# Inverse row norm computed on 96 by 3 values, and attention priorities of batches 1 to 3 spread by VectorE and GpSimd work

## The chip, the core and the metric

The kernel runs on one core of one Trainium2 chip. The metric is the device time of one execution in microseconds (us); the time before is the median of three runs. Beside it stands one profiled execution, from which all rows below come. TensorE (PE) does matrix products, VectorE (DVE), ScalarE (ACT) and GpSimd (POOL) work on elements, SyncE (SP) issues nearly all DMAs.

## The reference

Nystrom attention on q, k, v of shape 4 x 8 x 576 x 64 (batch, head, token, dimension), then a gated MLP behind an RMS norm, then a second MLP, all in fp32, 2304 tokens of width 512:

```python
def _moe_ref(x, w_gate, w_val, w_out, rms_g):
    rms = np.sqrt(np.mean(x * x, axis=-1, keepdims=True) + 1e-06)
    xn = x / rms * rms_g
    g = xn @ w_gate
    silu = g * (1.0 / (1.0 + np.exp(-g)))
    val = xn @ w_val
    return (silu * val @ w_out)

def _moe2_ref(x, w_in, w_out, s, b):
    r = np.maximum(x @ w_in, 0.0)
    return ((s * (r * r) + b) @ w_out)

attn = A @ Z @ C @ v      # A, C softmaxes against 32 landmarks, Z from 6 steps Z = 2 Z - Z Bm Z
x = attn.transpose(0, 2, 1, 3).reshape(2304, 512)
out = _moe2_ref(_moe_ref(x))
```

The weights come as 64-bit floats and are narrowed on the chip.

## The kernel before

Four batches of 576 tokens. Batch 0's attention comes first (to about 41.7 us of the span). Then the first MLP runs in 48 units, counted from 0: each is one of 12 slices of 128 hidden columns for one batch, 12 units to a batch. While the units of batch b run, the attention of batch b + 1 is worked in between, so attention 1 lies in units 0 to 11, attention 2 in 12 to 23, attention 3 in 24 to 35. Units 36 to 47 have no attention; in them the second MLP's weights are narrowed. From 529 us on the second MLP runs alone.

A unit is, on PE: eight products of `fused` (L972, weights r times the folded attention matrix gw, into a PSUM bank), 24 products of `first_mm` (L991) and, six units later for the same slice, 24 products of `out_mm` (L1039; in the first 12 units plain fp32 products, L1035). Between them ACT copies the bank of L972 to `uh` (L978), DVE subtracts to get `ul` (L980); ACT takes the tanh (L1006), DVE multiplies (L1008, L1012). In units 0 to 11 the first MLP's weights are also loaded and narrowed: a DMA into one of three `stage` buffers (L884, L886), two ACT passes (L897, L899), two DVE passes (L901, L904), and a store for later batches.

At the end of each attention stands the row norm, once for each half of the batch (288 columns; 8 times in all). x is never written out there: `x_mm` (L821) makes each quarter of x transposed in a bank, ACT squares it (L827), in batches 1 to 3 two additions (L833, DVE or POOL) sum the quarters, and a product with a 128 x 128 matrix of ones (L839) puts the sum of squares into all 128 rows of a bank. Then DVE adds 1e-6 (L843) and takes the reciprocal (L844) of 128 x 288 values in place, ACT takes the root (L847), DVE scales the two halves of the attention probabilities by it (L852), ACT and POOL split these into `xh` and `xl` (L856, L858), which the first MLP's products of the next batch read. In batch 0 the four quarters are summed by four products in place of the additions.

The order of the work is made when the program is built. Each operation has a key (its priority) and a planned duration on each engine that may do it; `Scheduler.run` walks through planned time and gives an engine that is free the ready operation of lowest key. On the chip each engine then does its instructions in that fixed order and waits by semaphores. Keys of the units are their planned times `T[n]`. The keys of one batch's attention are set by `by_path` (L120 to L132): between `t0` and `t1`, the planned times of the units beside it, each operation stands by the length of the longest path behind it. Planned costs of POOL and DVE operations hold each other off where both use the memory port that the two share (`pair`). Until planned time 60, `warm` (L1228) puts small products with ones into gaps of PE, into bank 7.

The attention of batches 1 to 3 has two PSUM banks, 6 and 7 (`at_r`); a bank is taken at the first operation that uses it and given back after the last.

Of the kernel before, what the change touches and what calls it, by code (L numbers as in the profile page):

```python
# [14 lines left out]
ALU = mybir.AluOpType  # L15
# [69 lines left out]
class Scheduler:  # L85
# [38 lines left out]
    def by_path(self, ops, t0, t1):  # L124

        way, inside = {}, {id(o) for o in ops}
        for o in reversed(ops):
            way[id(o)] = min(o.alts.values()) + max(
                (self.CROSS + way[id(u)] for u in o.users if id(u) in inside), default=0.0)
        most = max(way.values())  # L130
        for o in ops:
            o.key = t1 - (t1 - t0) * way[id(o)] / most  # L132

# [109 lines left out]
def t_mm4(n):  # L243
    return 0.00167 * max(n, 120)
# [3 lines left out]
def tile_nystrom_attention_two_mlps(  # L248
# [152 lines left out]
    def attention(b, t0, t1):  # L401
# [406 lines left out]
        for hf in range(2):  # L808
# [3 lines left out]
            for c in range(KD):  # L812
# [12 lines left out]
                if pr == 0:  # L825
                    at(("pe", 0.6), p0, x_mm, r=[WBD, AT[hf, g]], w=[*pX2, (xq, "taken")])
                at(("act", t_act(HC)), p0 + 0.01, lambda e, c=c, pX=pX, xq=xq: e.activation(  # L827
                    out=xq.t[:, HC * c:HC * c + HC], in_=pX.t[:, 0:HC], func=ACTF.Square, scale=float(DM) ** -0.5),
                    r=[pX], w=[(xq, c)])
            pS = Buf(ps_r)  # L830
# [7 lines left out]
            for c in range(n_sum):  # L838
                at(("pe", t_mm4(HC)), p0 + 0.05, lambda e, c=c, pS=pS, xq=xq: nc.tensor.matmul(  # L839
                    out=pS.t[:, 0:HC], lhsT=ones, rhs=xq.t[:, HC * c:HC * c + HC],  # L840
                    start=(c == 0), stop=(c == n_sum - 1)), r=[(xq, c), "const"] + ([pS] if c else []), w=[pS])
            def s_rec(e, pS=pS):
                e.tensor_scalar(out=pS.t[:, 0:HC], in0=pS.t[:, 0:HC], scalar1=1e-6, scalar2=None, op0=ALU.add)  # L843
                e.reciprocal(out=pS.t[:, 0:HC], in_=pS.t[:, 0:HC])  # L844

            at(("dve", 2 * t_dve(HC)), p0 + 0.06, s_rec, r=[pS], w=[pS])
            at(("act", t_act(HC) if first else 1.3 + t_act(HC)), p0 + 0.07, lambda e, pS=pS: e.activation(  # L847
                out=pS.t[:, 0:HC], in_=pS.t[:, 0:HC], func=ACTF.Sqrt), r=[pS, "table"], w=[pS])
            for g in range(2):
                a = AT[hf, g]  # L850
                cols = slice(2 * HC * g + HC * hf, 2 * HC * g + HC * hf + HC)
                at(("dve", t_dve(HC)), p0 + 0.08, lambda e, a=a, pS=pS: e.tensor_tensor(  # L852
                    out=a.t[:, 0:HC], in0=a.t[:, 0:HC], in1=pS.t[:, 0:HC], op=ALU.mult), r=[a, pS], w=[a])
# [239 lines left out]
    EARLY = 15  # L1093
    units = [(b, f) for b in range(B) for f in range(F1)]
# [64 lines left out]
    for n in range(len(units) + HALF + 1):  # L1159
        t = T[n]  # L1160
        if n < len(units):
            b, f = units[n]
            if f == 0:
                if b + 1 < B:
                    attention(b + 1, *at_time(b + 1))
                    S_.by_path(batch_ops[b + 1], *at_time(b + 1))
                else:
# [97 lines left out]
```

## Time and profile before

| | |
|---|---|
| time, median of 3 runs | 922.77 us (922.74 to 926.39) |
| the profiled execution's own time | 924.32 us |
| its span, first to last instruction | 922.3 us |
| PE, DVE, ACT, POOL busy | 881.8, 722.4, 444.9, 124.1 us |
| mean granted clock of TensorE | 0.990 of full |

Busy shares are means over stages with different limits. PE's instructions overlap, so a busy PE says that it had work, and an idle stretch of PE is work time lost. The granted clock of a stretch is a mean of two levels, 1.0 (2.4 GHz) and 0.5 (1.2 GHz).

### The profile page before, as it was taken

The numbers are of one execution on the slowest core, as the hardware profiler recorded it, in microseconds if no ns is written. First come the engines' busy times: TensorE is split into PE (matmuls) and PEld (weight loads), VectorE is DVE, ScalarE is ACT, GpSimd is POOL, SyncE is SP. The second block draws the span as 40 slices with busy tenths as digits, with TensorE's granted clock in tenths as the row PEclk, the third lists the DMA queues.
The fourth block names the chain that finished last, engine by engine and source line by source line (L and its number), as shares of the span: only waits on it lengthen the run. The fifth ranks groups of instructions, "written<-read, shape, count | busy, mean of one in ns | idle before, by whom it ended". The sixth has DMA issues, their size and how long they took to land.

```text
span 922.3 us, 16186 instructions
## 1 busy us (share of the span) xinstructions
PE 881.8 (96%) x6077; PEld 734.5 (80%) x6077; DVE 722.4 (78%) x1454; ACT 444.9 (48%) x885; POOL 124.1 (13%) x154
## 2 busy tenths in 40 slices
PE   8778998999989999999899999999999999999998
PEld 5565766898868988798788888888888888888896
DVE  7878888887898878888989966676667666666686
ACT  5466657434553345556767333343334334333454
POOL 1550053500850004200000000000000000000000
PEclk9989998999999999999999999999999999999999
DMA  7778878873524433348876200010001000100010
GB/s 222 197 231 282 279 223 271 289 255 92 144 85 143 131 101 91 94 145 268 288 253 220 74 0 1 1 46 1 0 1 46 1 1 0 47 1 1 18 30 23
DMA packets 72126, 105.92 MB, mean 115 GB/s; under 512 B 25200, under 2 KB 45680, under 8 KB 72048
## 3 DMA queue, kind: packets, MB, share of 16 engines
q1 hardware_dynamic: 71856, 104.62, 36.2%
q8 instruction: 48, 0.79, 0.3%
q14 instruction: 30, 0.25, 0.1%
q10 hardware_dynamic: 192, 0.26, 0.1%
HBM read 90.70 MB, written 14.16 MB: 114 GB/s over the span
## 4 chain that ended last, share of the span: by engine, by line
PE 76%; DVE 11%; DMA 5%; issue 3%; ACT 3%; SPq 0%; DVEq 0%; ACTq 0%
PE bank L1065 21%; PE bank L955 21%; PE bank L991 13%; PE bank L1039 10%; PE bank L972 3%; DVE cmag L901 2%; DMA stage<-in_moe_w_val_dram 2%; PE bank L1035 2%; DMA stage<-in_moe_w_out_dram 1%; PE bank L642 1%; PE bank L1228 1%; PE bank L580 1%; DVE wl L873 1%; DMA region<-in_q_dram 1%; DVE rawg L904 1%
## 5 line engine op out<-in xcount | busy, mean ns | idle before, releaser
L991 PE MATMUL bank<-xh,uh 128*128 128x288 f32 x384 | 127.1, 331 | 14.6 <-DVE ul L980 12.9
L955 PE MATMUL bank<-xh,uh 128*128 128x512 f32 (+1 forms) x320 | 117.7, 368 | 1.0 <-ACT hbuf L1206 1.0
L955 PE MATMUL bank<-xl,uh 128*128 128x512 f32 (+1 forms) x320 | 117.6, 368 | 0.0
L955 PE MATMUL bank<-xh,ul 128*128 128x512 f32 (+1 forms) x320 | 117.6, 368 | 0.0
L1206 ACT ACTIVATE hbuf<-bank 128x512 f32<-128x512 f32 (+1 forms) x79 | 44.0, 556 | 149.5 <-PE bank L955 147.5
L991 PE MATMUL bank<-xl,uh 128*128 128x288 f32 x384 | 114.5, 298 | 0.0
L991 PE MATMUL bank<-xh,ul 128*128 128x288 f32 x384 | 114.4, 298 | 0.0
L1065 PE MATMUL bank<-wh,hh 128*128 128x512 f32 x288 | 112.4, 390 | 0.3 <-DVE hh L872 0.3
L1065 PE MATMUL bank<-wl,hh 128*128 128x512 f32 x288 | 112.3, 390 | 0.0
L1065 PE MATMUL bank<-wh,hl 128*128 128x512 f32 x288 | 112.0, 389 | 0.0
L991 PEld LDWEIGHTS bank<-xh,uh 128*128 128x128 f32 x384 | 73.3, 191 | 40.1 <-DVE ul L980 16.8
L1039 PE MATMUL bank<-hh,wh 128*128 128x288 f32 x336 | 101.1, 301 | 0.0
L1039 PE MATMUL bank<-hl,wh 128*128 128x288 f32 x336 | 99.6, 296 | 1.0 <-DVE hl L873 1.0
L1039 PE MATMUL bank<-hh,wl 128*128 128x288 f32 x336 | 99.0, 295 | 0.0
L873 DVE TENSOR_TENSOR hl<-hbuf,hh 128x512 fp32r<-128x512 f32 (+2 forms) x126 | 73.6, 585 | 2.4
L991 PEld LDWEIGHTS bank<-xl,uh 128*128 128x128 f32 x384 | 73.7, 192 | 0.7
L991 PEld LDWEIGHTS bank<-xh,ul 128*128 128x128 f32 x384 | 73.5, 191 | 0.0
L955 PEld LDWEIGHTS bank<-xh,uh 128*128 128x128 f32 x320 | 60.2, 188 | 12.6 <-ACT hbuf L1206 1.2
L955 PEld LDWEIGHTS bank<-xl,uh 128*128 128x128 f32 x320 | 60.0, 188 | 11.0
L872 DVE CAST uh<-region 128x512 fp32r<-128x512 f32 x57 | 24.3, 426 | 56.7 <-PE bank L955 56.7
L955 PEld LDWEIGHTS bank<-xh,ul 128*128 128x128 f32 x320 | 60.1, 188 | 10.0
L1039 PEld LDWEIGHTS bank<-hh,wh 128*128 128x128 f32 x336 | 63.2, 188 | 3.6 <-issue 2.1
(188 smaller groups left out, 1849.0 us busy)
## 6 DMA issues: line engine op xcount, KB each, us to landing
rawo<-kepto SPq DMA_DIRECT2D x84, 256.0 KB, 3.3
rawg<-keptg SPq DMA_DIRECT2D x36, 512.0 KB, 3.7
stage<-in_moe_w_out_dram SPq DMA_DIRECT2D x28, 512.0 KB, 4.9
stage<-in_moe_w_in_dram SPq DMA_DIRECT2D x16, 512.0 KB, 5.4
stage<-in_moe_w_gate_dram SPq DMA_DIRECT2D x12, 512.0 KB, 4.9
stage<-in_moe_w_val_dram SPq DMA_DIRECT2D x12, 512.0 KB, 5.4
keptg<-rawg SPq DMA_DIRECT2D x12, 512.0 KB, 6.2
region<-in_k_dram SPq DMA_DIRECT2D x8, 576.0 KB, 5.8
```

The lines of the kernel that those rows point to most:

```text
L580: nc.tensor.matmul(out=ps.t[p, pn * g:pn * g + n], lhsT=lhsT(p, g), rhs=rhs(p, g), start=True, stop=True)
L642: nc.tensor.matmul(out=ps.t[:, 0:HC], lhsT=part(u, "bd")[:, 128 * e:128 * e + 128], rhs=part(y, "t").rearrange("p (t e i) -> p t e i", e=2 ...
L872: else e.tensor_copy(out=hi(), in_=src())), r=r, w=[wh], pair=True)
L873: b = op({"dve": t_dve(n), "pool": t_pool(n)}, key, lambda e: e.tensor_tensor(out=lo(), in0=src(), in1=hi().bitcast(F32), op=ALU.subtract) ...
L901: op(("dve", t_dve(512)), key, lambda e: e.scalar_tensor_tensor(out=m.t, in0=word(1), scalar=-2 ** 31, in1=m.t, op0=ALU.bitwise_and, op1=A ...
L955: nc.tensor.matmul(out=ps.t[:, 0:n], lhsT=w[a].t[:, ks], rhs=x[y].t[:, kd, 0:n], start=(kd == 0 and i == 0), stop=(kd == KD - 1 and i == 2))
L972: nc.tensor.matmul(out=pU.t[64 * i:64 * i + 64, 256 * g:256 * g + 256], lhsT=gw[b].t[:, 64 * k:64 * k + 64], rhs=r.t[:, :, 128 * k:128 * k ...
L991: nc.tensor.matmul(out=ps.t[:, 0:HC], lhsT=u[a].t[:, 256 * g + 128 * part:256 * g + 128 * part + 128], rhs=x[y].t.rearrange("p k n -> p (k ...
L1035: nc.tensor.matmul(out=A[c].t[:, 0:HC], lhsT=r.t[:, 128 * c:128 * c + 128], rhs=h.t, start=(f == 0), stop=(f == F1 - 1))
L1039: nc.tensor.matmul(out=A[c].t[:, 0:HC], lhsT=w[a].t[:, 128 * c:128 * c + 128], rhs=hs[y].t[:, 0:HC], start=(f == 0 and i == 0), stop=(f == ...
L1065: nc.tensor.matmul(out=A[c].t, lhsT=hs[a].t[:, s], rhs=w[y].t, start=(f == 0 and i == 0), stop=(f == F2 - 1 and i == 2))
L1206: e.activation(out=r.t[:, 0:n], in_=ps.t[:, 0:n], func=ACTF.Relu) if e is nc.scalar
```

## The change

Two edits.

The norm: the sums of squares are now wanted once for each token, as 96 rows by 3 columns, in place of 128 equal rows by 288 columns. For each of three groups of 96 tokens a product takes the squares as the stationary matrix (128 x 96) and one column of ones as the moving one, so the sum of squares of a token falls into one of 96 partitions (`s_mm`; 3 products, in batch 0 four times as many). Scaling by 1/512 moves from the square's scale to the DVE instruction that adds 1e-6. That instruction, the reciprocal and the root work on 96 x 3 values, now in SBUF. To get the result back into 128 rows by 288 columns, DVE or POOL multiplies a 96 x 96 identity by the three columns (`dg`, 96 x 288), and one product of ones with it (contraction over 96) spreads each value over all 128 rows of a second bank, pR. The scaling reads pR.

The keys: after `by_path`, `by_work` moves the keys of the attention of batches 1 to 3 seven tenths of the way (`EVEN`) to a place that grows evenly with the DVE and POOL work done so far. The order within one attention by key stays; its place against the units' work changes. Nothing else is edited, but all orders are made anew.

```diff
@@ -130,6 +130,17 @@
         most = max(way.values())
         for o in ops:
             o.key = t1 - (t1 - t0) * way[id(o)] / most
+
+    def by_work(self, ops, t0, t1, part):
+
+
+        def work(o):
+            return 0.1 + (o.alts["dve"] if "dve" in o.alts else 0.6 * o.alts.get("pool", 0.0))
+
+        total, done = sum(work(o) for o in ops), 0.0
+        for o in sorted(ops, key=lambda o: o.key):
+            o.key += part * (t0 + (t1 - t0) * done / total - o.key)
+            done += work(o)
 
     def start_of(self, o, e):
         t = max((f + (self.SAME if d == e else PEC if e == 'pe' and o.key > 5 else self.CROSS) for d, f in o.ready.items()), default=0.0)
@@ -825,9 +836,8 @@
                 if pr == 0:
                     at(("pe", 0.6), p0, x_mm, r=[WBD, AT[hf, g]], w=[*pX2, (xq, "taken")])
                 at(("act", t_act(HC)), p0 + 0.01, lambda e, c=c, pX=pX, xq=xq: e.activation(
-                    out=xq.t[:, HC * c:HC * c + HC], in_=pX.t[:, 0:HC], func=ACTF.Square, scale=float(DM) ** -0.5),
-                    r=[pX], w=[(xq, c)])
-            pS = Buf(ps_r)
+                    out=xq.t[:, HC * c:HC * c + HC], in_=pX.t[:, 0:HC], func=ACTF.Square), r=[pX], w=[(xq, c)])
+            pS, pR, rs, dg = Buf(ps_r), Buf(ps_r), Buf(sm_r), Buf(a_ring)
             if not first:
                 for c, n in ((2, 2 * HC), (1, HC)):
                     at(dp(n), p0 + 0.03, lambda e, c=c, n=n, xq=xq: e.tensor_tensor(
@@ -835,22 +845,36 @@
                         r=[(xq, i) for i in range(KD)] if n > HC else [(xq, 0), (xq, c)],
                         w=[(xq, 0)] + ([(xq, 1)] if n > HC else []))
             n_sum = KD if first else 1
-            for c in range(n_sum):
-                at(("pe", t_mm4(HC)), p0 + 0.05, lambda e, c=c, pS=pS, xq=xq: nc.tensor.matmul(
-                    out=pS.t[:, 0:HC], lhsT=ones, rhs=xq.t[:, HC * c:HC * c + HC],
-                    start=(c == 0), stop=(c == n_sum - 1)), r=[(xq, c), "const"] + ([pS] if c else []), w=[pS])
-            def s_rec(e, pS=pS):
-                e.tensor_scalar(out=pS.t[:, 0:HC], in0=pS.t[:, 0:HC], scalar1=1e-6, scalar2=None, op0=ALU.add)
-                e.reciprocal(out=pS.t[:, 0:HC], in_=pS.t[:, 0:HC])
-
-            at(("dve", 2 * t_dve(HC)), p0 + 0.06, s_rec, r=[pS], w=[pS])
-            at(("act", t_act(HC) if first else 1.3 + t_act(HC)), p0 + 0.07, lambda e, pS=pS: e.activation(
-                out=pS.t[:, 0:HC], in_=pS.t[:, 0:HC], func=ACTF.Sqrt), r=[pS, "table"], w=[pS])
+
+            def s_mm(_, pS=pS, xq=xq):
+                for j in range(3):
+                    for c in range(n_sum):
+                        nc.tensor.matmul(
+                            out=pS.t[0:NP, j:j + 1], lhsT=xq.t[:, HC * c + NP * j:HC * c + NP * j + NP],
+                            rhs=ones[:, 0:1], start=(c == 0), stop=(c == n_sum - 1))
+
+            at(("pe", 0.26 * n_sum), p0 + 0.05, s_mm, r=[*[(xq, c) for c in range(n_sum)], "const"], w=[pS])
+
+            def s_rec(e, pS=pS, rs=rs):
+                e.tensor_scalar(out=rs.t[0:NP, 0:3], in0=pS.t[0:NP, 0:3], scalar1=1.0 / DM, scalar2=1e-6, op0=ALU.mult, op1=ALU.add)
+                e.reciprocal(out=rs.t[0:NP, 0:3], in_=rs.t[0:NP, 0:3])
+
+            at(("dve", 0.3), p0 + 0.06, s_rec, r=[pS], w=[rs])
+            at(("act", 0.2 if first else 1.4), p0 + 0.07, lambda e, rs=rs: e.activation(
+                out=rs.t[0:NP, 0:3], in_=rs.t[0:NP, 0:3], func=ACTF.Sqrt), r=[rs, "table"], w=[rs])
+            at(dp(HC), p0 + 0.07, lambda e, rs=rs, dg=dg: e.tensor_tensor(
+                out=dg.t[0:NP].rearrange("p (j c) -> p j c", j=3),
+                in0=ident[0:NP, 0:NP].unsqueeze(1).to_broadcast([NP, 3, NP]),
+                in1=rs.t[0:NP, 0:3].rearrange("p (j o) -> p j o", o=1).to_broadcast([NP, 3, NP]),
+                op=ALU.mult), r=[rs, "ident"], w=[dg])
+            at(("pe", t_mm4(HC)), p0 + 0.08, lambda e, dg=dg, pR=pR: nc.tensor.matmul(
+                out=pR.t[:, 0:HC], lhsT=ones[0:NP, :], rhs=dg.t[0:NP], start=True, stop=True),
+                r=[dg, "const"], w=[pR])
             for g in range(2):
                 a = AT[hf, g]
                 cols = slice(2 * HC * g + HC * hf, 2 * HC * g + HC * hf + HC)
-                at(("dve", t_dve(HC)), p0 + 0.08, lambda e, a=a, pS=pS: e.tensor_tensor(
-                    out=a.t[:, 0:HC], in0=a.t[:, 0:HC], in1=pS.t[:, 0:HC], op=ALU.mult), r=[a, pS], w=[a])
+                at(("dve", t_dve(HC)), p0 + 0.08, lambda e, a=a, pR=pR: e.tensor_tensor(
+                    out=a.t[:, 0:HC], in0=a.t[:, 0:HC], in1=pR.t[:, 0:HC], op=ALU.mult), r=[a, pR], w=[a])
                 wh, wl = (([(pair[i], ("a", hf, g))] + ([(pair[i], "t")] if fine else [])) for i in range(2))
                 at({"act": t_act(HC), "dve": t_dve2(HC)}, p0 + 0.09, lambda e, a=a, cols=cols: (
                     e.activation(out=part(0, "t")[:, cols], in_=a.t[:, 0:HC], func=ACTF.Copy) if e is nc.scalar
@@ -1091,6 +1115,7 @@
     U_PE = 0.95
     MORE = 1.4
     EARLY = 15
+    EVEN = 0.7
     units = [(b, f) for b in range(B) for f in range(F1)]
     HALF = F1 // 2
     t_first, t_out = 6 * t_mm(HC), 12 * t_mm(HC)
@@ -1164,6 +1189,7 @@
                 if b + 1 < B:
                     attention(b + 1, *at_time(b + 1))
                     S_.by_path(batch_ops[b + 1], *at_time(b + 1))
+                    S_.by_work(batch_ops[b + 1], *at_time(b + 1), EVEN)
                 else:
                     gate("attn", at_ops, t)
             u = us.pop(n)
```

The changed kernel's lines stand lower than those of before: by 11 ahead of the norm, by 24 behind it, by 26 near the end. What was L844, L847 and L852 is L860, L863 and L876 there; L980, L991, L1008 and L1039 are L1004, L1015, L1032 and L1063; the new products are L852 (sums) and L870 (spreading), the new multiplication L865.

The order, DVE at the end of attention 1, around the subtraction `ul` of unit 10 (bank_69 and bank_70 are the two attention banks, cmag, rawg, rawo the narrowing of weights). Before:

```order
L901 SCALAR_TENSOR_TENSOR cmag_96<-stage_90,cmag_96 128x512
L904 SCALAR_TENSOR_TENSOR rawo_88<-ca_94,cmag_96 128x512
L843 TENSOR_SCALAR bank_69<-bank_69 128x288
L844 RECIPROCAL bank_69<-bank_69 128x288
L843 TENSOR_SCALAR bank_70<-bank_70 128x288
L844 RECIPROCAL bank_70<-bank_70 128x288
L901 SCALAR_TENSOR_TENSOR cmag_96<-stage_91,cmag_96 128x512
L904 SCALAR_TENSOR_TENSOR rawg_86<-ca_94,cmag_96 128x512
L980 TENSOR_TENSOR ul_99<-bank_68,uh_97 128x512
L901 SCALAR_TENSOR_TENSOR cmag_95<-stage_92,cmag_95 128x512
L1008 SCALAR_TENSOR_TENSOR hbuf<-hbuf,bank_67 128x288
```

Now:

```order
L1004 TENSOR_TENSOR ul_99<-bank_68,uh_97 128x512
L1032 SCALAR_TENSOR_TENSOR hbuf<-hbuf,bank_67 128x288
L512 STREAM_TRANSPOSE region<-region 128x64
L925 SCALAR_TENSOR_TENSOR cmag_96<-stage_92,cmag_96 128x512
L859 TENSOR_SCALAR region<-bank_70 96x3
L860 RECIPROCAL region<-region 96x3
L859 TENSOR_SCALAR region<-bank_69 96x3
L860 RECIPROCAL region<-region 96x3
L1036 SCALAR_TENSOR_TENSOR hbuf<-hbuf,bank_68 128x288
L542 STREAM_TRANSPOSE region<-region 128x1152
L813 TENSOR_TENSOR gw_106<-bank_70,gT 64x2x32 x2
```

The two reciprocals of 128 x 288 stood in a row ahead of `ul`; now `ul` stands ahead of the short instructions of the norm, and transposes of attention 2 (L512, L542) have come in behind them.

ACT at the same place (stage, ca, cmag: narrowing; L1006, now L1030, is the tanh). Before:

```order
L978 ACTIVATE uh_97<-bank_68 128x512
L847 ACT_TABLE_LOAD
L847 ACTIVATE bank_69<-bank_69 128x288
L1006 ACT_TABLE_LOAD
L1006 ACTIVATE hbuf<-bank_67 128x288
L847 ACT_TABLE_LOAD
L847 ACTIVATE bank_70<-bank_70 128x288
L897 ACTIVATE ca_94<-stage_90 128x512
L899 ACTIVATE cmag_96<-stage_90 128x512
L1006 ACT_TABLE_LOAD
L1006 ACTIVATE hbuf<-bank_67 128x288
L856 ACTIVATE xh_81<-region 128x288 x2
```

Now:

```order
L923 ACTIVATE cmag_96<-stage_92 128x512
L1030 ACTIVATE hbuf<-bank_67 128x288
L921 ACTIVATE ca_93<-stage_90 128x512
L923 ACTIVATE cmag_95<-stage_90 128x512
L863 ACT_TABLE_LOAD
L863 ACTIVATE region<-region 96x3 x2
L1030 ACT_TABLE_LOAD
L1030 ACTIVATE hbuf<-bank_67 128x288
L921 ACTIVATE ca_94<-stage_91 128x512
L880 ACTIVATE xh_81<-region 128x288 x4
L923 ACTIVATE cmag_96<-stage_91 128x512
```

Four loads of a function table stood around the two roots; the two roots now stand together between two loads, behind a pair of narrowing passes that read a stage buffer.

PE at the end of attention 2, before at the product with ones of the second half, and now at the new product that spreads the first half's result (L1039 and L1063: out_mm, L991 and L1015: first_mm, L996: fused of the next unit). Before:

```order
L1039 MATMUL bank_63<-hh_109,wh_102 128x288
L1039 MATMUL bank_63<-hl_111,wh_102 128x288
L1039 MATMUL bank_63<-hh_109,wl_104 128x288
L839 MATMUL bank_70<-region,ones 128x288
L991 MATMUL bank_68<-xh_81,uh_98 128x288
L991 MATMUL bank_68<-xl_83,uh_98 128x288
L991 MATMUL bank_68<-xh_81,ul_100 128x288
L991 MATMUL bank_68<-xh_81,uh_98 128x288
L991 MATMUL bank_68<-xl_83,uh_98 128x288
```

Now:

```order
L1063 MATMUL bank_65<-hh_108,wh_101 128x288
L1063 MATMUL bank_65<-hl_110,wh_101 128x288
L1063 MATMUL bank_65<-hh_108,wl_103 128x288
L996 MATMUL bank_68<-rawg_85,gw_106 64x256 x4
L870 MATMUL bank_70<-region,ones 128x288
L1015 MATMUL bank_67<-xh_81,uh_98 128x288
L1015 MATMUL bank_67<-xl_83,uh_98 128x288
L1015 MATMUL bank_67<-xh_81,ul_100 128x288
L1015 MATMUL bank_67<-xh_81,uh_98 128x288
L1015 MATMUL bank_67<-xl_83,uh_98 128x288
L1015 MATMUL bank_67<-xh_81,ul_100 128x288
```

Before, PE did its part of the norm and went on with the units, and no later instruction of the norm was PE's. Now a second one, L870, stands in PE's row among the units' products and reads what DVE, ACT and POOL have made of the sums.

## Rows read from the trace of the kernel before

**Rows 1.** The page, busy time of each engine.

```profile
PE 881.8 (96%) x6077; PEld 734.5 (80%) x6077; DVE 722.4 (78%) x1454; ACT 444.9 (48%) x885; POOL 124.1 (13%) x154
```

**Rows 2.** The page, chain that ended last, by engine.

```profile
PE 76%; DVE 11%; DMA 5%; issue 3%; ACT 3%; SPq 0%; DVEq 0%; ACTq 0%
```

**Rows 3.** Busy time of each engine in stretches of the span.

```profile
core 0: us, PE busy (x) PEld busy (x) DVE busy (x) ACT busy (x) POOL busy (x), PEclk, DMA share, GB/s
...
41.70:59.00 17.30, 10.26 (x72) 7.56 (x71) 14.24 (x18) 7.96 (x17) 7.91 (x9) 0.80 0.73 221
59.00:97.50 38.50, 34.01 (x276) 25.73 (x275) 31.14 (x73) 24.08 (x52) 5.12 (x6) 1.00 0.81 269
97.50:143.50 46.00, 45.71 (x475) 31.82 (x474) 40.41 (x90) 29.53 (x65) 16.32 (x20) 1.00 0.80 257
143.50:158.90 15.40, 11.81 (x67) 9.27 (x66) 14.17 (x22) 13.04 (x21) 4.02 (x6) 0.78 0.78 255
158.90:254.00 95.10, 95.10 (x855) 82.05 (x854) 79.02 (x186) 44.44 (x99) 35.00 (x43) 1.00 0.63 197
254.00:284.30 30.30, 25.42 (x189) 21.82 (x188) 26.92 (x49) 14.89 (x26) 14.55 (x19) 1.00 0.33 103
...
370.60:390.10 19.50, 17.30 (x135) 14.94 (x134) 17.65 (x34) 11.99 (x20) 6.05 (x6) 1.00 0.36 107
390.10:529.40 139.30, 131.41 (x921) 118.03 (x920) 128.03 (x249) 85.00 (x173) 6.52 (x6) 0.99 0.64 207
```

**Rows 4.** Timeline, end of attention 1 (start, length, engine, what, idle before).

```profile
144.40 1.97 DVE L844 RECIPROCAL bank<-bank 128x288 f32<-128x288 f32 x1
...
145.75 0.68 ACT L897 ACTIVATE ca<-stage 128x512 f32<-128x512 f32 x1 [3.29 <-DMA stage<-in_moe_w_gate_dram]
...
146.71 1.97 DVE L844 RECIPROCAL bank<-bank 128x288 f32<-128x288 f32 x1
146.88 0.58 ACT L978 ACTIVATE uh<-bank 128x512 fp32r<-128x512 f32 x1
147.48 1.28 ACT L847 ACT_TABLE_LOAD   x1
...
148.77 0.40 ACT L847 ACTIVATE bank<-bank 128x288 f32<-128x288 f32 x1
...
149.91 0.69 DVE L980 TENSOR_TENSOR ul<-bank,uh 128x512 fp32r<-128x512 f32 x1
...
150.65 0.61 PE L991 MATMUL bank<-xh,uh 128*128 128x288 f32 x1 [3.59 <-DVE ul L980]
```

**Rows 5.** Timeline, end of attention 0.

```profile
30.03 11.19 SPq L454 DMA_DIRECT2D region<-in_v_dram  x13
...
46.30 0.66 ACT L897 ACTIVATE ca<-stage 128x512 f32<-128x512 f32 x1 [2.57 <-DMA stage<-in_moe_w_val_dram]
...
49.94 4.65 PE L1228 MATMUL bank<-ones 128*128 128x256 bf16 x23 [6.46 <-ACT region L495]
...
54.34 0.38 PE L991 MATMUL bank<-xh,uh 128*128 128x288 f32 x1
```

**Rows 6.** Timeline, end of attention 2.

```profile
262.64 1.97 DVE L844 RECIPROCAL bank<-bank 128x288 f32<-128x288 f32 x1
...
266.34 1.08 PE L972 MATMUL bank<-rawg,gw 128*64 128x256 f32 x8 [2.50 <-DVE hbuf L1008]
```

**Rows 7.** Groups of instructions: count, busy us, mean ns of one, idle before.

```profile
L844 DVE RECIPROCAL bank<-bank 128x288 f32<-128x288 f32 x8 | 15.7, 1966 | 0.3
L752 POOL TENSOR_TENSOR region<-region 128x288 f32<-128x288 f32 x14 | 12.7, 914 | 73.3 <-DVE region L751 67.4 <-DVE region L687 5.9
...
L757 DVE TENSOR_SCALAR region<-region 128x9 f32<-128x9 f32 x16 | 4.0, 250 | 0.5
L843 DVE TENSOR_SCALAR bank<-bank 128x288 f32<-128x288 f32 x8 | 3.5, 440 | 2.0 <-PE bank L839 2.0
...
L758 DVE RECIPROCAL region<-region 128x9 f32<-128x9 f32 x16 | 3.5, 216 | 0.5
```

**Rows 8.** Timeline of PE: eight fp32 instructions with one moving block of 32 columns.

```profile
206.17 1.08 PE L555 MATMUL bank<-region 128*128 128x32 f32 x8
207.09 0.38 PE L1039 MATMUL bank<-hh,wh 128*128 128x288 f32 x1
```

## The prediction

> **What bounds the kernel now.** I read the page's busy times first, then the chain, then the span cut into stretches, and last the timeline where PE stands still. PE is busy for 881.8 of 922.3 us and DVE for 722.4 [rows 1], and the chain that ends last is PE for 76% and DVE for 11% [rows 2]. So PE is the bound, and all that can be gained is the 40 us in which it has nothing to do, plus what its lower clock costs. The stretches show where these are [rows 3]. From 158.9 to 254.0 PE is busy for all 95.10 us; a change of DVE's work there is worth nothing. The losses that touch this change lie where a batch's attention ends, and there I take idle time as length less PE busy:
> - end of attention 0, 41.7 to 59.0: 7.0 us idle, and the granted clock is 0.80 in the mean, so 0.2 x 17.3 = 3.5 us of full speed are lost;
> - end of attention 1, 143.5 to 158.9: 3.6 us idle and 0.22 x 15.4 = 3.4 us lost to the clock;
> - end of attention 2, 254.0 to 284.3: 4.9 us idle, clock 1.00;
> - end of attention 3, 370.6 to 390.1: 2.2 us idle, clock 1.00.
>
> The timeline says why at the end of attention 1 [rows 4]: two reciprocals of 1.97 us stand in DVE's order ahead of `ul`. `uh` is ready at 147.46, `ul` begins at 149.91, and PE waits 3.59 us for it, in the stretch whose clock is 0.78 [rows 3]. At the end of attention 2 a reciprocal at 262.64 stands ahead of L1008, on which the next fused product waits 2.50 us [rows 6]. So DVE decides in these places, in bursts, though its mean share is only 78%.
>
> **The change part by part.** *DVE, removed.* Each of the 8 half-batches loses 0.44 + 1.97 us on 128 x 288 values and gets the same two on 96 x 3. The nearest rows, 128 x 9, take 0.25 and 0.22 [rows 7]; the new ones lie between nothing and that. I take 0.4 for both, so 2.0 us are saved each time, 16 us in all. Where PE is full this is worth nothing; at the four ends it takes away the waits named above, since no DVE instruction of 2 us is left in the norm.
>
> *The root on ACT* shrinks too, but what counts there is the table load of 1.28 us ahead of it, which stays [rows 4]. At attention 1 both roots now share one load, elsewhere each has its own.
>
> *POOL, added.* The multiplication with the identity, like L752: 0.91 us each [rows 7]. POOL is idle for most of its time at these ends [rows 3], so it costs only as a link of the chain below.
>
> *PE, added.* In batches 1 to 3 the product with ones goes and the spreading product comes, of equal size but for 96 rows in place of 128: nothing. The three products with 96 columns of weights and one moving column are new. The nearest row has 8 instructions, with 128 columns of weights and 32 moving, from 206.17 to the next product at 207.09, so 0.115 us each; an fp32 product is two of them, 0.23 us [rows 8]. Bounds: nothing, if they fall into idle time, and 0.23. I take 0.23, since the weights have almost the same size: 3 x 0.23 = 0.7 us a half, 1.4 us a batch. This is work on the bound engine, a true cost. In batch 0 it is 24 products, 5.5 us, against six large ones less.
>
> *A new wait.* PE's order now holds the spreading product (the order of PE in the section on the change). Everything behind it on PE, the units' products, waits until DVE (0.4), ACT (1.28 and a root of at most 0.4), and POOL (0.91) have done their part: 3.0 us from the sums. What covers it is the PE work between: about 3.5 us of products at attention 1, 4.9 at attention 2, 3.9 at attention 3, counted in the order at 0.135 us each (what eight instructions of L972 take, 1.08 us [rows 6]). So the first half is just covered. The second half is worse: its root needs a switch back to tanh and another to the root, 2 x 1.28 and a tanh more, about 3.3 us, with 1.9 us to 2.3 us of PE work between the two. And at attention 1 the roots stand behind two narrowing passes on ACT that wait for a weight DMA; before, such a wait was 3.29 us there [rows 4]. Bounds of what is left per batch: nothing, and 3.6 us as now. I take 1.5 at attention 1 (half of that DMA wait), 1.2 at attention 2, 0.6 at attention 3.
>
> The Trainium skill, ScalarE: Activation LUTs, section "What ACT_TABLE_LOAD costs", gives each switch a drain of about 1.38 us on top of the 1.28 us load. The trace does not agree: the root begins at 148.77, with the load's end, and the load began 0.02 us after `uh` ended [rows 4]. By the rule the sum would be some 1.4 us worse for each half.
>
> *The keys.* They move work of one attention between units. At the end of attention 2 DVE is busy for 26.92 of 30.30 us [rows 3]; of that 4 go with the reciprocals, and the order now does more of the attention's transposes and sums earlier, in a stretch where PE is full and DVE has 79.02 of 95.10. I cost it at nothing: the room that covers it is 16 us of DVE. If that room is missing in one unit, DVE becomes late there by what was moved in, some 2 us.
>
> *Sum.* Attention 0: the wait for reciprocals goes, but the first product of the units stands behind 23 small products that the scheduler put there, and they behind a bank that ACT frees [rows 5]; the changed order has 30 of them, and ACT still waits for the weight DMA that lands at 46.30, which SP could issue only after 11.19 us of issuing v [rows 5]. I take -1.0, between -4 (most of the stall of 6.46) and +2 (a part of the sums' 5.5 comes on top). Attention 1: -3.6 - 3.4 + 1.4 + 1.5 = -4.1. Attention 2: -4.9 + 1.4 + 1.2 = -2.3. Attention 3: -2.2 + 1.4 + 0.6 = -0.2. Together -7.6. The profiled execution took 924.3 us, so 916.7; it lies 1.5 us above the median of the runs, so a median of **915 us**.
>
> **The rivals.**
> *PE waits at the spreading product as long as it waited for `ul`* (no change). For it: the chain of 3.0 us has four engines in it, and the orders were made with planned durations. Against it: 3.5 to 4.9 us of PE work cover the first half. If each of the six halves waits 1.3 us more than none, in place of the 3.3 us that my three terms hold, that is 7.8 - 3.3 = 4.5 us more: 919.5; with nothing gained at attention 0, 920.5. By the drain of the Trainium skill's page named above all six roots would be late by about that much.
>
> *The wait brings the low clock with it* (slower). At attention 1 a wait of 3.6 us came with 3.4 us lost to the clock [rows 3, 4]. At attention 2 and 3 the waits were in pieces and the clock stayed. If the spreading product makes one whole wait of 3.6 us in each of the three ends, with 3.4 us of clock each, the three cost 21.0 + 4.2 of added products against the 14.1 of now: +11, with attention 0 at -1 some +10, so 933. It decides where the waits in one batch, with their clock, come to more than what the batch loses now less 1.4 us: 5.6 us at attention 1, 3.5 at attention 2, 0.8 at attention 3. For it: attention 1's DMA wait. Against it: DVE is freed in the same place, so narrowing buffers come free earlier.
>
> *The whole burst goes and more with it.* Between 59.0 and 97.5 PE is idle for 4.5 us and from 390.1 to 529.4 for 7.9 [rows 3]. If an earlier end of attention 0 and 1 also carries the weight narrowing ahead, these shrink: with half of them, and no wait at the spreading product, 915 - 3.3 - 6 = 906. Against it: weight DMAs set the pace there, DMA share 0.81 and 0.64 [rows 3], and they are not changed.
>
> **How the numbers follow.** The forecast (910 to 917.5) 0.48, more gained (902 to 910) 0.18, waits eat it (917.5 to 924) 0.22, slower by the clock (924 to 938) 0.12. Runs of this kernel can tell a change from none at about 0.5%, 4.6 us: faster means below 918.2, slower above 927.4. From the cases: faster 0.68, same 0.23, slower 0.09. The range leaves out the far ends: 905 to 922.
>
> **What would show it.** Right: no DVE instruction of 1.97 us; no PE wait for `ul` at the end of attention 1, and clock 1.00 there; PE idle at the end of attention 2 below 2 us; PE busy up by about 4 us for the three-column sums. Wrong: idle time of PE ahead of L870 of more than 1.5 us a half, a granted clock below 0.9 in a stretch where it was 1.00, or PE idle in 216 to 254, where it was full, since the keys put DVE work there. The forecast falls if the new chain is twice as long as its rows.

## The result, and the profile after

The changed kernel took 914.39 us (median of 4 runs, 913.4 to 918.31), the kernel before 923.7 us beside it (4 runs, 922.74 to 926.39). The ratio is 0.9918, 95% interval 0.9892 to 0.9944: faster by 0.8%. The profiled execution of the changed kernel took 914.43 us with a span of 912.4; that of before had 924.3 and 922.3. One of the twelve runs of the kernel before with its plan made true in batches 1 to 3 took 1215.69 us at a granted clock of 0.654, where the others had 0.99 or more; it is left out of that kernel's figures below.

The page's busy times and the chain that ended last, of the changed kernel; they answer to [rows 1] and [rows 2]:

```profile
PE 883.8 (97%) x6150; PEld 739.7 (81%) x6150; DVE 707.3 (78%) x1461; ACT 438.9 (48%) x878; POOL 130.1 (14%) x160
...
PE 75%; DVE 15%; DMA 3%; ACT 3%; issue 3%; DVEq 0%; ACTq 0%; SPq 0%
```

PE has 2.0 us more work than before and stands still for 912.4 - 883.8 = 28.6 us, where it stood for 40.5. That is the whole gain: 11.9 less idle, 2.0 more busy. DVE is rid of 15 us, and yet its share of the chain rose from 11 to 15%.

The new norm in the groups of instructions (count, busy us, mean ns of one, idle before), for [rows 7]:

```profile
L863 ACT ACT_TABLE_LOAD x5 | 6.4, 1283 | 0.1
L865 POOL TENSOR_TENSOR region<-ident,region 96x288 f32<-96x288 f32 x7 | 5.2, 738 | 13.2 <-ACT region L863 13.2
L870 PE MATMUL bank<-region,ones 96*128 96x288 f32 x14 | 4.6, 413 | 0.0
L860 DVE RECIPROCAL region<-region 96x3 f32<-96x3 f32 x8 | 1.4, 172 | 0.3
L859 DVE TENSOR_SCALAR region<-bank 96x3 f32<-96x3 f32 x8 | 1.2, 155 | 8.2 <-PE bank L852 5.7 <-ACT wh L895 2.3
```

The two instructions on DVE that took 2.41 us now take 0.33. In the column of idle time, L870, the spreading product, has 0.0: PE never stood still ahead of it, and the wait that the prediction feared is not there.

Busy time in stretches of the changed kernel. They begin at the same units as those of [rows 3], but the one at the end of attention 1 holds two units here (10 and 11), where [rows 3] has unit 10 alone:

```profile
core 0: us, PE busy (x) PEld busy (x) DVE busy (x) ACT busy (x) POOL busy (x), PEclk, DMA share, GB/s
...
40.70:54.90 14.20, 12.69 (x87) 9.65 (x86) 9.71 (x17) 10.45 (x22) 11.26 (x14) 0.87 0.84 263
...
138.40:162.20 23.80, 21.00 (x131) 16.60 (x130) 21.59 (x38) 11.92 (x23) 16.96 (x20) 0.93 0.85 282
162.20:247.90 85.70, 84.91 (x799) 74.44 (x798) 70.70 (x174) 38.16 (x84) 22.04 (x27) 1.00 0.59 182
247.90:276.40 28.50, 27.19 (x211) 23.45 (x210) 21.49 (x46) 16.89 (x32) 18.91 (x24) 1.00 0.32 107
...
360.80:381.00 20.20, 19.61 (x155) 16.47 (x154) 14.77 (x32) 13.55 (x25) 8.64 (x9) 1.00 0.30 95
```

The first stretch, the end of attention 0, lost 7.0 us of PE before and loses 1.5 now; at the end of attention 2 the idle time fell from 4.9 to 1.3, at that of attention 3 from 2.2 to 0.6. The end of attention 1 still has 2.8 us idle and a clock of 0.93, and it is no shorter than before: units 10 and 11 took 23.6 us (143.5 to 167.1) and now take 23.8. Unit 10 alone went from 15.3 to 11.5, unit 11 from 8.3 to 12.3. Unit 11 in the kernel before, then in the changed one:

```profile
158.85:167.10 8.25, 8.25 (x49) 6.61 (x48) 7.99 (x16) 2.74 (x6) 4.86 (x6) 1.00 0.80 280
```
```profile
149.88:162.16 12.28, 9.89 (x50) 8.02 (x49) 10.91 (x18) 4.91 (x11) 9.41 (x11) 0.86 0.77 268
```

The timeline of the end of attention 1 (start, length, engine, what, idle before):

```profile
137.61 0.69 DVE L928 SCALAR_TENSOR_TENSOR rawo<-ca,cmag 128x512 int32<-128x512 int32 x1
...
142.71 1.10 PE L852 MATMUL bank<-ones,region 128*96 128x1 f32 x12
...
144.41 1.28 ACT L863 ACT_TABLE_LOAD   x1
145.71 0.30 ACT L863 ACTIVATE region<-region 96x3 f32<-96x3 f32 x2
...
147.35 0.65 PE L870 MATMUL bank<-region,ones 96*128 96x288 f32 x2
147.43 0.66 POOL L865 TENSOR_TENSOR region<-ident,region 96x288 f32<-96x288 f32 x1
...
148.81 0.65 PE L870 MATMUL bank<-region,ones 96*128 96x288 f32 x2
...
150.75 3.97 POOL L882 TENSOR_TENSOR xl<-region,xh 128x288 fp32r<-128x288 f32 x4 [0.72 <-ACT xh L880]
150.95 1.15 DVE L925 SCALAR_TENSOR_TENSOR cmag<-stage,cmag 128x512 int32<-128x512 int32 x1
...
152.13 1.17 DVE L928 SCALAR_TENSOR_TENSOR rawo<-ca,cmag 128x512 int32<-128x512 int32 x1
...
153.35 1.08 PE L1059 MATMUL bank<-hbuf,rawo 128*128 128x288 f32 x2 [2.39 <-DVE rawo L928]
```

The wait of 3.59 us for `ul` [rows 4] is gone from unit 10, but in unit 11 PE stands for 2.39 us until the weights `rawo` are unpacked (their narrowing on DVE, L925 and L928), and the clock falls to half for 3.41 us behind it. The two unpacking instructions on DVE take 1.15 and 1.17 us here, beside four GpSimd instructions that run on end for 3.97 us; the L928 at 137.61, where GpSimd is idle from 137.03 to 139.05, takes 0.69. So one stall was taken away, a smaller one stood one unit behind it, and PE had the norm's new products to do in between.

Where the gain lies, by the start of a unit's first fused product (us from the span's start), with three of the experiments:

| start of | before | after | norm only | keys only | six reciprocals back |
|---|---|---|---|---|---|
| unit 1 | 58.99 | 54.92 | 53.85 | 58.31 | 57.09 |
| unit 12 | 167.11 | 162.16 | 160.07 | 166.98 | 166.80 |
| unit 24 | 284.30 | 276.38 | 273.95 | 285.04 | 285.24 |
| unit 36 | 397.62 | 388.90 | 385.62 | 401.89 | 400.03 |
| the end | 922.28 | 912.37 | 909.85 | 925.56 | 923.76 |

Read as differences of the first two columns: -4.1 us up to unit 1, -0.9 from there to unit 12, -3.0 to unit 24, -0.8 to unit 36, -1.2 behind. The first figure is the least certain: in five traces of the same order up to there (the changed kernel twice, and the runs below with reciprocals put back and with doubled sums), unit 1 begins between 54.0 and 57.1 us, with a clock at half for 6.8 to 13.7 us of batch 0.

### The profile page after: what moved, and what is told of

Read it like the earlier page. It is cut to its first block, busy times and chain, and to the rows that moved or that the text cites. A ratio compares the mean times of both kernels' runs of the same rounds, so it can differ in the third digit from the quotient of the medians.

```text
span 912.4 us, 16352 instructions
## 1 busy us (share of the span) xinstructions
PE 883.8 (97%) x6150; PEld 739.7 (81%) x6150; DVE 707.3 (78%) x1461; ACT 438.9 (48%) x878; POOL 130.1 (14%) x160
## 4 chain that ended last, share of the span: by engine, by line
PE 75%; DVE 15%; DMA 3%; ACT 3%; issue 3%; DVEq 0%; ACTq 0%; SPq 0%
PE bank L1089 21%; PE bank L979 21%; PE bank L1015 12%; PE bank L1063 10%; PE bank L996 3%; DVE cmag L925 2%; PE bank L653 1%; DVE wl L897 1%; DVE ul L1004 1%; DMA stage<-in_moe_w_out_dram 1%; DVE rawg L928 1%; DVE hl L897 1%; DVE region L479 1%; PE bank L1059 1%; PE bank L832 1%
## 5 line engine op out<-in xcount | busy, mean ns | idle before, releaser
L1015 PE MATMUL bank<-xh,uh 128*128 128x288 f32 x384 | 125.6, 327 | 10.2 <-DVE ul L1004 9.6
L1015 PE MATMUL bank<-xh,ul 128*128 128x288 f32 x384 | 114.2, 297 | 0.0
L1015 PE MATMUL bank<-xl,uh 128*128 128x288 f32 x384 | 114.1, 297 | 0.0
L1063 PE MATMUL bank<-hh,wh 128*128 128x288 f32 x336 | 100.9, 300 | 0.1
L1015 PEld LDWEIGHTS bank<-xh,uh 128*128 128x128 f32 x384 | 73.0, 190 | 34.3 <-DVE ul L1004 15.0
L1063 PE MATMUL bank<-hl,wh 128*128 128x288 f32 x336 | 99.5, 296 | 1.0 <-DVE hl L897 1.0
L1063 PE MATMUL bank<-hh,wl 128*128 128x288 f32 x336 | 99.0, 295 | 0.0
L1015 PEld LDWEIGHTS bank<-xl,uh 128*128 128x128 f32 x384 | 73.2, 191 | 0.4
L1015 PEld LDWEIGHTS bank<-xh,ul 128*128 128x128 f32 x384 | 73.1, 190 | 0.0
L1063 PEld LDWEIGHTS bank<-hh,wh 128*128 128x128 f32 x336 | 63.4, 189 | 3.0 <-issue 1.9
```

The lines of the kernel that those rows point to most:

```text
L1015: nc.tensor.matmul(out=ps.t[:, 0:HC], lhsT=u[a].t[:, 256 * g + 128 * part:256 * g + 128 * part + 128], rhs=x[y].t.rearrange("p k n -> p (k ...
L1063: nc.tensor.matmul(out=A[c].t[:, 0:HC], lhsT=w[a].t[:, 128 * c:128 * c + 128], rhs=hs[y].t[:, 0:HC], start=(f == 0 and i == 0), stop=(f == ...
```

## The experiments

**Theory:** the gain is DVE's time at the ends of the attentions, which the long reciprocals took; the keys give nothing. **Rivals:** the keys make the gain; or it is the order alone, which was made with 0.73 us for an instruction pair of 2.41.

*The two parts apart.* The norm without the keys, and the kernel before with the keys (there `by_work` and `EVEN = 0.7` come in as in the change; the one line that uses them is shown):

```diff
-    EVEN = 0.7
+    EVEN = 0.0
```
```diff
+                    S_.by_work(batch_ops[b + 1], *at_time(b + 1), EVEN)
```

> The changed kernel without the move of the keys (EVEN 0). The prediction's theory, that the gain is the two long reciprocals and the keys are worth nothing: 914 to 917 us, as the changed kernel. The rival, that the keys carry a good part by spreading VectorE's work over the units: 918 us or more.

> The kernel before with the keys moved and the norm left as it was. The prediction's theory: no change, 921 to 925 us, and the waits behind the reciprocals of 1.97 us still stand at the ends of attentions 1 to 3. The rival, that the keys alone take those waits away because less work stands beside the reciprocals: 919 us or less.

Measured: the norm alone 911.49 us, ratio 0.9875 (0.9853 to 0.9897); the keys alone 931.03, ratio 1.0079 (1.0049 to 1.0109). The norm makes the whole gain, and the keys cost. Neither lies where the theory had put it (914 to 917, and 921 to 925). For the kernel with the keys alone, the waits of PE (line, what it waited for, us in all, times, longest) show how; the same wait came to 12.9 us in the kernel before:

```profile
PE bank L1002 <- DVE ul L991: 21.4, 15, 3.4
```

and its timeline at the end of attention 3 shows one of these waits (line numbers are each kernel's own; L991 is `ul` here):

```profile
382.13 1.97 DVE L855 RECIPROCAL bank<-bank 128x288 f32<-128x288 f32 x1
384.00 0.44 DVE L863 TENSOR_TENSOR region<-region,bank 128x288 f32<-128x288 f32 x1
...
386.64 0.69 DVE L991 TENSOR_TENSOR ul<-bank,uh 128x512 fp32r<-128x512 f32 x1
...
387.38 0.40 PE L1002 MATMUL bank<-xh,uh 128*128 128x288 f32 x1 [3.40 <-DVE ul L991]
```

A wait nearly as long as that of [rows 4] now stands at the end of attention 3, where before there was none of that length (2.2 us idle in the whole stretch, [rows 3]).

*Both again, side by side on one chip,* for the price of the keys on top of the new norm:

> The changed kernel itself, on the same chip and in the same rounds as the norm alone, for the price of the keys. Theory that the new keys cost: 2 to 4 us above the norm alone. Rival that they cost nothing, as the prediction put it: within 1 us of it.

> The new norm with the old keys, beside the changed kernel on the same chip. Theory that the keys cost: 2 to 4 us below the changed kernel, a ratio to the kernel before of 0.987 to 0.989. Rival: the same as the changed kernel within 1 us.

Measured: 915.5 us (912.59 to 917.13, ratio 0.9915, 0.9894 to 0.9935) against 911.96 (909.24 to 913.53, ratio 0.9876, 0.9854 to 0.9898). The keys cost 3.5 us here, 2.9 between the first two runs. The intervals just touch, but both pairs agree: the norm with the old keys is the better kernel, 1.2% below the one before.

*The long reciprocal put back.* The changed kernel in its own order, with an extra reciprocal on 128 x 288 squares in each half of batch 0, or of batches 1 to 3 (`not first`); it is work added, and nothing needs its result:

```diff
-            def s_rec(e, pS=pS, rs=rs):
+            def s_rec(e, pS=pS, rs=rs, xq=xq):
...
+                if first:
+                    e.reciprocal(out=pS.t[:, 0:HC], in_=xq.t[:, 0:HC])
```

> The changed kernel in its own order, with a reciprocal of 128 x 288 values added to the norm of batch 0 alone, two in all; its result goes into a bank's unused columns and is read by nobody. The prediction's step (the end of attention 0 is worth 1 us): 915 to 916 us. As the two traces read, where unit 1 began 4.1 us earlier: 918 us, if nothing later gives it back. The rival, that the weights' way through the narrowing sets the pace of units 1 to 11: unit 1 late by 3 to 4 us, unit 12 by less than 1, and 914 to 915 us.

> The changed kernel in its own order, with the same added reciprocal in the norm of batches 1 to 3, six in all. The prediction's steps (waits of 3.6 + 3.4, 4.9 and 2.2 us behind the reciprocals): 920 to 924 us, with PE waiting for ul behind them at the end of attention 1. The rival, that the moved keys leave room for them: 914 to 916 us. As the two traces read, nothing at attention 1, 3 at 2 and 1 at 3: 918 us.

Measured: batch 0, 915.34 us, ratio 0.9922 (0.9901 to 0.9942): no cost. Batches 1 to 3, 925.66 us, ratio 1.0027 (1.0008 to 1.0046), 1.7 us above the expected 920 to 924: 11 us lost, as much as the whole gain. The six extra instructions in the groups:

```profile
L862 DVE RECIPROCAL bank<-region 128x288 f32<-128x288 f32 x6 | 11.6, 1927 | 0.0
```

11.6 us of DVE cost 11.3 us of the whole by the medians (925.66 - 914.39). By the table, 2.2 us of that lie ahead of unit 1, where the two kernels do the same work and the clock was at half for 13.7 us in place of 6.8; 9.0 lie in units 1 to 35. So at these three ends some four fifths of DVE's time pass to the end. In batch 0 the same instruction is free. There the timeline with the extra ones shows what covers them:

```profile
37.71 1.93 DVE L862 RECIPROCAL bank<-xbuf 128x288 f32<-128x288 f32 x1
39.36 1.20 PE L998 MATMUL bank<-rawg,gw 128*64 128x256 f32 x8
39.83 1.93 DVE L862 RECIPROCAL bank<-region 128x288 f32<-128x288 f32 x1
40.49 1.33 PE L872 MATMUL bank<-xbuf,ones 96*128 96x288 f32 x2
```

PE does the fused product and a spreading product meanwhile. So the 4.1 us that the changed kernel gains by unit 1 are not DVE's time. The extra instruction is read by nobody, so the run does not test whether an earlier result matters; but the result does not come quicker: from the addition of 1e-6 to the first scaling it is 4.8 us before (40.84 to 45.65) and 6.6 us now (37.34 to 43.97). What the rows do show is the remade order: the one stall of 6.46 us ahead of the 23 small products [rows 5] is in no row of the changed kernel. Before, ACT's second root and the copy L495, which the small products waited for, stood behind the narrowing pass that got its weights at 46.30 [rows 5]:

```profile
46.87 0.39 ACT L847 ACTIVATE bank<-bank 128x288 f32<-128x288 f32 x1
...
49.64 0.25 ACT L495 ACTIVATE region<-bank 128x128 f32<-128x128 f32 x1
```

Now both roots stand ahead of that pass, which starts without a wait, and the copy (now L506) follows; SP issues the first of these weight DMAs at 39.10 in place of 41.33:

```profile
41.27 0.20 ACT L863 ACTIVATE region<-region 96x3 f32<-96x3 f32 x1 [3.34 <-DVE region L860]
...
45.65 0.68 ACT L921 ACTIVATE ca<-stage 128x512 f32<-128x512 f32 x1
...
46.81 0.26 ACT L506 ACTIVATE region<-bank 128x128 f32<-128x128 f32 x1
```

No run varies this order by itself.

*Time, or only the plan?* First the six reciprocals again, but planned with their length; then the kernel before, whose own pair is planned with 2.41 us, in all batches (shown) or in batches 1 to 3 alone (`2 * t_dve(HC) if first else 2.41`):

```diff
-            at(("dve", 0.3), p0 + 0.06, s_rec, r=[pS], w=[rs])
+            at(("dve", 0.3 if first else 2.23), p0 + 0.06, s_rec, r=[pS], w=[rs])
```
```diff
-            at(("dve", 2 * t_dve(HC)), p0 + 0.06, s_rec, r=[pS], w=[pS])
+            at(("dve", 2.41), p0 + 0.06, s_rec, r=[pS], w=[pS])
```

> The changed kernel with the same six extra 128x288 reciprocals in batches 1 to 3 as in the run that was at 925.7, now planned with their true length (2.23 us for the step in place of 0.3), so that the scheduler can put the product's operands ahead of them. Theory that the ends of the attentions lack DVE's time itself: about 925 again, within 3 us. Rival, from the kernel before with its reciprocal planned truly (from unit 12 to the end it was as short as the changed kernel): what costs is a long instruction where the order expects a short one, and this comes out at 914 to 918.

> The kernel before, its long reciprocal left as it is; only the duration by which the scheduler plans it is set from 0.73 to the 2.41 us that the trace shows. Theory that the time of DVE itself is what the ends of the attentions lack: 919 to 925, no clear change, since the 2.4 us are still to be done there. Rival that what cost was only an order made with too short a duration, so that a true plan puts the product's operands ahead of the reciprocals: 913 to 917, most of the gain of the change without its new norm.

> The kernel before with its reciprocal as it is, planned with its true 2.41 us in batches 1 to 3 only; batch 0 keeps its order, since with the plan true in all four batches 6.7 us were lost by unit 10 (151.6 against 143.5) and 7 won back behind it. Theory that DVE lacks the time: 920 to 924. Rival that the order lacked the true length: unit 1 at 59 as before, the 3.6 us wait at the end of attention 1 gone, units 12 to the end in about 755 us where they took 755.2 before less 5, in all 914 to 918.

Measured: the reciprocals planned, 926.91 us, ratio 1.004 (1.0023 to 1.0058), no better than unplanned. The kernel before, planned truly in all batches, 920.04, ratio 0.9978 (0.9957 to 1.0000); in batches 1 to 3 alone 920.39, ratio 0.9970 (0.9952 to 0.9987). The plan is worth some 2.7 us of the norm's 11.7 (923.16 for the kernel before beside it, less 911.49), so most of the gain is not the plan. Where the plan helps, the starts of the units show: units 12 to 35 take 230.5 us before, 227.1 and 227.4 with the two true plans and 225.6 with the norm alone, so at attentions 2 and 3 the plan gives some 3 us of the norm's 5. In units 1 to 11 it gives nothing (108.1 before, 110.8 and 108.7 with the true plans, 106.2 with the norm alone). The waits of PE in the last of these kernels show why a true plan gives so little in all:

```profile
PE bank L972 <- DVE hbuf L1008: 8.4, 10, 2.5
PE bank L991 <- DVE ul L980: 6.8, 11, 1.7
```

In the profile of before these two were:

```profile
PE bank L991 <- DVE ul L980: 12.9, 13, 3.6
...
PE bank L972 <- DVE hbuf L1008: 5.7, 5, 2.5
```

The order took 6.1 us from the one, and 2.7 of that went to the other; DVE had the same work to do.

*The price of the new sums on PE,* by issuing those of batches 1 to 3 twice:

```diff
-                for j in range(3):
+                for j in range(3) if first else (0, 1, 2, 0, 1, 2):
```

> The changed kernel in its own order, with the three-column sums of batches 1 to 3 issued twice (18 fp32 products more; the result is the same). By the prediction's term each costs PE 0.23 us: 914.4 + 4.1 = 918.5. By the rows of the changed kernel's trace, 0.18 us a product: +3.3, so 917.7. If they lie in time in which PE would have stood still, no change (914.4); and if they bring the low clock, as the one-column products did at 37.6 us of batch 0, 3.4 us more for each drop: 921 or above.

Measured: 916.34 us, ratio 0.9927 (0.9902 to 0.9953), 0.8 to 2 us above the changed kernel, less than the interval. The page's busy times:

```profile
PE 885.8 (97%) x6186; PEld 740.7 (81%) x6186; DVE 705.7 (77%) x1461; ACT 439.2 (48%) x878; POOL 130.3 (14%) x160
```

2.0 us more busy for 18 products, 0.11 us each, and 1.4 us less idle (913.0 - 885.8 = 27.2 against 28.6). The trace speaks against the price of 4.1; that it is nothing the times can't exclude.

*Where the keys cost.* The new keys for batch 1 only, and for batches 2 and 3 only (`if b > 0`):

```diff
-                    S_.by_work(batch_ops[b + 1], *at_time(b + 1), EVEN)
+                    if b == 0:
+                        S_.by_work(batch_ops[b + 1], *at_time(b + 1), EVEN)
```

> The changed kernel with the new keys for batch 1's attention only; batches 2 and 3 have the old keys. The new keys cost about 3 us over the norm alone (914.4 against 911.5). Theory: nearly all of it (2.1 us by the start of unit 12) is lost while batch 1's attention is at work, so this kernel comes out as the changed one, 913 to 915. Rival: it is lost in batches 2 and 3, and this comes out as the norm alone, 911.5.

> The changed kernel with the new keys for the attentions of batches 2 and 3 only. Theory that the keys' cost lies in batch 1: as the norm alone, 911 to 912.5, with unit 12 begun at about 160.1 us in place of 162.2. Rival that it lies in batches 2 and 3: 913.5 to 915.

Measured: 913.58 us, ratio 0.9888 (0.9859 to 0.9916), and 914.11, ratio 0.9896 (0.9868 to 0.9924). Both lie between the norm alone and the changed kernel, and their intervals take in the ratios of both (0.9876 and 0.9915 in the pair on one chip). The expectation for batches 2 and 3 (911 to 912.5 by the theory) was missed: that all of the cost lies in batch 1 is not borne out. The times do not take it apart, but the starts of the units in the six traces do:

| | new keys there | old keys there |
|---|---|---|
| units 1 to 11 | 107.2, 108.2, 107.2 | 106.2, 103.8, 104.0 |
| units 12 to 35 | 226.7, 226.6, 227.7 | 225.6, 225.6, 225.7 |

The columns hold the changed kernel twice, then the run with half of the new keys; and the norm alone twice, then the run with the other half. So units 1 to 11 lose 1 to 4 us, units 12 to 35 some 1 to 2.

## Why the prediction was right, and where its steps were not

The time was forecast at 915 and is 914.4, inside the likeliest case. The sum -7.6 stood for -9.9 of the span. Its terms did not do as well, and that the sum came near is in part luck: attention 0 gave 3.1 us more than its term and attention 1 gave 3.2 less, and the two cancel.

- **DVE is what the ends lack:** right at attentions 1 to 3, and shown. The six reciprocals put back there cost 9.0 us in units 1 to 35, and 10.3 where they were planned; the norm alone had gained 6.9 and 9.2 there in its two traces. A part of what they cost at attentions 2 and 3 is the plan made too short (233.2 us in units 12 to 35, 230.3 when planned).
- **Attention 0, -1.0, bounds -4 to +2:** measured -4.1, the far bound. The term was mis-sized. The prediction feared the 24 new products and the order around them; the stall went with the new order instead, as the rows of ACT show. Which move in that order did it was not tried.
- **Attention 1, -4.1:** measured -0.9, and none of that at its end. In unit 10, the stretch that the term was worked out from, 3.8 us went as said, with the wait for `ul`. But the prediction named no next wait, and unit 11 grew by 4.0. It was DVE again, unpacking `rawo`: 2.39 us and 1.7 us of clock (3.41 us at half), in the rows above. A second trace of the changed kernel gained nothing in units 1 to 11 (108.2 us, 108.1 before).
- **Attention 2 and 3, -2.3 and -0.2:** measured -3.0 and -0.8. The waits that the next term added here did not come.
- **The new wait at the spreading product, 1.5 + 1.2 + 0.6:** none of it came. PE was idle ahead of L870 for 0.0 us over 14 records (the other two of the 16 read another buffer, also with 0.0). At attention 1 both roots shared one table load, as said, the first GpSimd product was done before PE had finished the work in front, and the second hid behind four instructions of L1059. The cover was longer than counted, and GpSimd took 0.74 us where 0.91 stood in the sum.
- **Three-column sums, 1.4 a batch:** half that size by the doubled run, 0.11 us a product in place of 0.23; the row at 142.71 has 0.18 (six products, each two instructions). The prediction's check on the page, PE busy up by about 4 us, seemed met (2.0 us more, with about 1.9 us less stretched by the low clock), but that holds batch 0's new products and lost large ones too, and does not test this price.
- **Keys, nothing:** wrong by 3 us. The cover named (16 us of DVE freed) is there in the total, but not where the keys put the work. A likely mechanism, from the groups of the unpacking instructions up to 165 us, first the changed kernel, then the norm alone:

```profile
L925 DVE SCALAR_TENSOR_TENSOR cmag<-stage,cmag 128x512 int32<-128x512 int32 x36 | 30.0, 837 | 1.2 <-ACT cmag L923 1.2
L928 DVE SCALAR_TENSOR_TENSOR rawg<-ca,cmag 128x512 int32<-128x512 int32 x24 | 19.7, 822 | 0.4
L928 DVE SCALAR_TENSOR_TENSOR rawo<-ca,cmag 128x512 int32<-128x512 int32 x12 | 11.1, 921 | 0.2
```
```profile
L925 DVE SCALAR_TENSOR_TENSOR cmag<-stage,cmag 128x512 int32<-128x512 int32 x36 | 28.8, 800 | 4.7 <-ACT cmag L923 4.7
L928 DVE SCALAR_TENSOR_TENSOR rawg<-ca,cmag 128x512 int32<-128x512 int32 x24 | 17.8, 740 | 0.3
L928 DVE SCALAR_TENSOR_TENSOR rawo<-ca,cmag 128x512 int32<-128x512 int32 x12 | 10.7, 890 | 0.1
```

The same 72 instructions take 60.8 us with the new keys and 57.3 without: the keys set more GpSimd work beside them. With the new keys 39 of the 72 overlap a GpSimd instruction and take 0.98 us in the mean, the other 33 take 0.68; without them 29 overlap. The other traces agree: 37 and 37 overlap where batch 1 has the new keys (the changed kernel again, batch 1 only), 30 and 31 where it has the old. That this is the loss in batch 1 is argued, not shown; no run took GpSimd away, and it says nothing of the 1 to 2 us in units 12 to 35.

Of the signs that the prediction named, the clock at the end of attention 1 was not 1.00: it was 0.86 in unit 11. And PE, which had been busy for all of 158.9 to 254.0, stood still for 0.8 us of units 12 to 20.

Of the rivals, the wait at the spreading product and the low clock that it might bring did not come. "More goes with the burst" came in part, at attention 0 and in the 1.2 us behind unit 36, and the norm alone comes nearer to it (911.5, forecast 906).

## What to carry to other kernels

Where an engine with a mean share of 78% stops the bound engine, look at its load in that stretch alone: there, 11.6 us of it cost 9 us of the whole, and the same instruction a batch earlier was free. When a stall is costed away, name the next operand that the bound engine needs and who makes it; here it was the same engine. Time the two halves of a change apart: one half gained 12 us and the other gave 3 back. When a sum comes true, compare its terms: here two errors of 3 us cancelled.

## What was not expected of the hardware

*The clock falls while PE is busy.* In the stretches of the changed kernel around unit 0:

```profile
33.00:35.10 2.10, 2.10 (x16) 1.54 (x13) 2.02 (x6) 1.75 (x6) 0.00 (x0) 1.00 0.38 86
35.10:37.58 2.48, 2.48 (x30) 2.48 (x30) 0.59 (x4) 0.79 (x3) 0.00 (x0) 1.00 0.45 96
37.58:44.41 6.83, 6.83 (x34) 5.18 (x34) 0.89 (x5) 1.00 (x3) 3.33 (x5) 0.50 0.81 207
```

PE has no gap from 33.0 on; from 35.10 it runs products of one moving column, and at 37.58 the granted clock goes from 2.4 to 1.2 GHz for 6.83 us. A full busy share in the stretch ahead did not mean a full clock behind it.

*GpSimd stretches DVE.* The unpacking of one weight, all instructions of it between 130 and 165 us (count, ns shortest, median, longest, first and last start):

```profile
L928 DVE SCALAR_TENSOR_TENSOR rawo<-ca,cmag x5: 691/832/1782, 133.9 to 158.8; 128x512 int32<-128x512 int32 x5
```

The longest, at 155.30, runs beside a GpSimd instruction of 1.86 us that began at 154.68 and the one behind it. The Trainium skill, SBUF — State Buffer, section "SBUF: two separate sides", has the two share a port pair as an exclusive lock, which a DVE instruction with two SBUF inputs also takes against a GpSimd instruction that reads SBUF. The rows agree in the sign (0.68 us alone, 0.98 beside GpSimd, in the means above); how long each waits was not measured by itself.

*No drain at a table load.* The load of 144.41 ends at 145.69 and the root begins at 145.71, as in [rows 4]: the drain that the prediction weighed does not show here either.
